# Float32 products for the first two chunks, unsplit until later, and weights first in the queue: attention and rational feed-forward on one core

## The chip, the core and the metric

The kernel runs on one core of a Trainium2 chip. Its engines are TensorE (PE in the profile, its weight loads PEld), VectorE (DVE), ScalarE (ACT), GpSimd (POOL) and SyncE (SP, which issues all transfers). Each runs its own list of instructions in order. The metric is device time in microseconds: the median of three runs before the change is 1022.39 us (1021.11 to 1024.19).

## The reference

```python
# q, k, v: 8 batches x 8 heads x 576 positions x 64;  w_in 512 x 2048;  w_out 2048 x 512
scores = q @ k.T / sqrt(64);  only positions rel in [0, 64) back count (window 64)
x = softmax(scores) @ v                     # heads side by side: 4608 tokens x 512
h = x @ w_in                                # 4608 x 2048
P = a[0] + a[1]*h + a[2]*h**2 + a[3]*h**3
Q = 1 + abs(b[0])*abs(h) + abs(b[1])*h**2
out = (P / (Q + 1e-6)) @ w_out              # 4608 x 512
```

The weights arrive as 64-bit floats, seen by the kernel as pairs of 32-bit words.

## The kernel before, in words

**Tiling.** The 4608 tokens are cut into 12 chunks of 384 (`CH`). A chunk's attention is done in four units, one for each pair of heads: `unit_load` (transfers of q, k, v), `unit_scores` (scores in PSUM, mask and scale on VectorE, exponentials on ScalarE, one scaling by the reciprocal sums: `sm`), `unit_transpose` (`pT`), `unit_av` (the product with v in PSUM `ps_x`, copied to `x`). The 2048 hidden columns are cut into 16 blocks. One block of one chunk is a step: `ffn1` multiplies the chunk's `x` (four tiles of 128 x 384) with a block of `w_in` into `h`, then works out the gate P/Q on ScalarE, VectorE and, from the 29th gate on (`DEC`), one operation on GpSimd; `ffn2` multiplies the gate with a block of `w_out` and adds it up in three PSUM tiles `o` of 128 x 512 over all steps of a chunk. `ffn2` runs three steps behind `ffn1` (`LAG`).

**Order of steps.** Steps 0 to 7 are the first 8 blocks of chunk 0, steps 8 to 15 the same of chunk 1, 16 to 23 the second half of chunk 1, 24 to 31 the second half of chunk 0. The half sum of chunk 0 is therefore set aside after step 7 (three copies to `part`, line 287, on ScalarE) and added at the end of step 31. From step 32 on each chunk takes 16 steps, to step 191.

**Products in parts.** Every operand is split into a high part rounded to `float32r` and a low part, the rest. A product is made of three `float32r` matmuls: high by low, high by high, low by high. So a step has 12 first products (128 x 384) and 9 second ones (128 x 512). `x` is split in `unit_av` (a cast on ScalarE, a subtraction on VectorE, `xl`), the gate by three more operations on VectorE, the weights by `decode`.

**Decoding weights.** `decode` loads a tile of 512 KB into a staging buffer `w_st` (two of them) and turns 64-bit floats into 32-bit ones: an absolute value on ScalarE (line 113), a maximum, a shift, two merges on VectorE (lines 114 to 118), then the split: a cast on ScalarE (line 121) and a subtraction on VectorE (line 122). There are 16 tiles of `w_in` and 16 of `w_out`. Four `w_in` tiles are loaded while the first chunk's units are done; the others are called step by step from a table, `todo`, which is filled by `at(step, function, ...)`.

**What sets the order.** The program is written step by step, but a scheduler of the framework then sets the order of each engine's instructions by its own estimate of times. Since each engine works in order, an instruction that waits holds all behind it on its engine.

Of the kernel before, what the change touches and what calls it, by code (L numbers as in the profile page):

```python
# [20 lines left out]
DEC = 28  # L21
AHEAD = 3
LAG = 3
W_AT = 0, 1, 2, 3
WLEAD = len(W_AT)
# [6 lines left out]
def swa_rational_ffn(ctx: ExitStack, tc: tile.TileContext, qT, kT, v, w_in, w_out, a, b, out):  # L32
# [17 lines left out]
    xp = ctx.enter_context(tc.tile_pool(name="xp", bufs=2))  # L50
    tmp = ctx.enter_context(tc.tile_pool(name="tmp", bufs=2))
    gp = ctx.enter_context(tc.tile_pool(name="gp", bufs=LAG + 1))
    op = ctx.enter_context(tc.tile_pool(name="op", bufs=2))
# [13 lines left out]
    def make_mask():  # L67
        nc.gpsimd.memset(mask, BIG)
        for j in range(NM):
            for half in range(2):  # L70
# [23 lines left out]
    wi_h = const.tile([P, NCC, DFF], F32R, name="wi_h")  # L94
    wi_l = const.tile([P, NCC, DFF], F32R, name="wi_l")
    wo_h = const.tile([P, NF, DO], F32R, name="wo_h")
    wo_l = const.tile([P, NF, DO], F32R, name="wo_l")
# [3 lines left out]
    def decode(src, hi, lo):  # L101

        w = stage.tile([P, 512, 2], U32, name="w_st", bufs=2)
        if len(src.shape) == 3:
            nc.sync.dma_start(out=w.rearrange("p (c n) two -> p c (n two)", c=src.shape[1]), in_=src)
        else:
            nc.sync.dma_start(out=w.rearrange("p n two -> p (n two)"), in_=src)
        low, high = w[:, :, 0], w[:, :, 1]
        c = stage.tile([P, 512], U32, name="w_c")
        cf = c.bitcast(F32)  # L110


        nc.scalar.activation(cf, w.bitcast(F32)[:, :, 1], AF.Abs)
        nc.vector.tensor_scalar(out=cf, in0=cf, scalar1=2.0 ** -15, scalar2=None, op0=ALU.max)

        nc.vector.tensor_scalar(out=c, in0=c, scalar1=3, scalar2=0x3FFFFFF8, op0=ALU.logical_shift_left, op1=ALU.bitwise_and)
        nc.vector.scalar_tensor_tensor(out=c, in0=low, scalar=29, in1=c, op0=ALU.logical_shift_right, op1=ALU.bitwise_or)  # L117
        nc.vector.scalar_tensor_tensor(out=c, in0=high, scalar=0xC0000000, in1=c, op0=ALU.bitwise_and, op1=ALU.bitwise_or)  # L118
        if len(hi.shape) == 3:
            cf = cf.rearrange("p (c n) -> p c n", c=hi.shape[1])  # L120
        nc.scalar.copy(out=hi, in_=cf)
        nc.vector.tensor_tensor(out=lo, in0=cf, in1=hi.bitcast(F32), op=ALU.subtract)

    def load_w_in(i):
        sl = slice(i * P, (i + 1) * P)
        decode(w_in_v[:, :, 2 * i * P:2 * (i + 1) * P], wi_h[:, :, sl], wi_l[:, :, sl])

    def load_w_out(i):
        decode(w_out_v[:, i, :], wo_h[:, i, :], wo_l[:, i, :])
# [87 lines left out]
    def unit_av(c, hp):  # L217
# [7 lines left out]
        xh[c, hp] = xp.tile([P, CH], F32R, name=f"xh{hp}")  # L225
        xl[c, hp] = xp.tile([P, CH], F32R, name=f"xl{hp}")
        x = ps.rearrange("p t s -> p (t s)")
        nc.scalar.copy(out=xh[c, hp], in_=x)
# [5 lines left out]
    def ffn1(c, i):  # L234
        h = ps_h.tile([P, CH], F32, name="h")
        n = 0
        for cc in range(NCC):
            for w, x in ((wi_h, xl), (wi_h, xh), (wi_l, xh)):
                nc.tensor.matmul(h, w[:, cc, i * P:(i + 1) * P], x[c, cc], start=n == 0, stop=n == 3 * NCC - 1)  # L239
                n += 1  # L240
# [3 lines left out]
        gh = gp.tile([P, CH], F32R, name="gh")  # L244
        gl = gp.tile([P, CH], F32R, name="gl")
# [8 lines left out]

        nc.scalar.activation(ah, u, AF.Ln, bias=QADD)
        nc.scalar.activation(ah, ah, AF.Exp, scale=-1.0)  # L256
        nc.vector.scalar_tensor_tensor(out=gh, in0=num, scalar=a_sb[:, 0:1], in1=ah, op0=ALU.add, op1=ALU.mult)  # L257
# [12 lines left out]
    def ffn2(s):  # L270
# [6 lines left out]
        for t in range(NTS):  # L277
            ts = slice(t * P, (t + 1) * P)
            for n, (g, w) in enumerate(((gl, wo_h), (gh, wo_l), (gh, wo_h))):
                nc.tensor.matmul(acc[c][t], g[:, ts], w[:, i, :], start=first and n == 0, stop=last and n == 2)  # L280
# [3 lines left out]
        if c == 0 and c not in part:  # L284
            part[c] = const.tile([P, NTS, DO], F32, name="part")
            for t in range(NTS):
                nc.scalar.copy(out=part[c][:, t, :], in_=o[t])
            return
        for t in range(NTS):
            ob = part[0][:, t, :] if s == total - 1 else op.tile([P, DO], F32, name="ob")  # L290
            if c in part:
                nc.vector.tensor_tensor(out=ob, in0=o[t], in1=part[c][:, t, :], op=ALU.add)
# [15 lines left out]
    wi, wo = list(range(H, NF)), list(range(H, NF))  # L308
    queue = [(load_w_in, wi.pop(0)) for _ in range(WLEAD)]
    while wi or wo:  # L310
        if wi:
            queue.append((load_w_in, wi.pop(0)))
        queue.append((load_w_out, wo.pop(0)))
    for n, call in enumerate(queue):
        at(H + n - 1, *call)

# [16 lines left out]

    for k in range(NU + 2):
# [7 lines left out]
        if k in W_AT:  # L342
            load_w_in(W_AT.index(k))
# [45 lines left out]
```

## Time and profile before

| | |
|---|---|
| median of three runs | 1022.39 us |
| profiled execution, its own time | 1025.14 us |
| its span | 1023.3 us |
| TensorE busy | 953.1 us (93%) |
| VectorE busy | 850.3 us (83%) |
| ScalarE busy | 725.8 us (71%) |
| GpSimd busy | 233.7 us (23%) |
| transfers | 64.09 MB, mean 63 GB/s |
| mean granted TensorE clock | 0.978 |

Busy shares are means over stages with different limits, so they are read by stretches of time. In rows of single instructions the columns are the start and the length in us, then engine, line, operation, output and inputs with their shapes, and how many such instructions follow each other (x24). An instruction's length overlaps the next one's; the cost of one in a full queue is the distance from its start to the next start. In the rows of groups the numbers behind the bar are the sum of busy time and the mean length in ns.

### The profile page before, as it was taken

How to read it: one execution, taken by the hardware profiler on the slowest of the kernel's cores; microseconds unless marked ns; L12 is line 12 of the kernel's file. 1: busy time of each engine (PE TensorE's matmuls, PEld its weight loads, DVE VectorE, ACT ScalarE, POOL GpSimd, SP SyncE). 2: the span in 40 equal slices, each digit the busy share in tenths (PEclk: the TensorE clock that was granted, in tenths of full speed). 3: DMA queues.
4: the chain of work that ended last, by engine and by line, in shares of the span. 5: the costliest groups of instructions: out<-in, count | busy, mean ns of one | idle time of the engine just before them, and what ended most of it. 6: DMA issues, size and time to landing. Idle time of an engine off the chain costs nothing.

```text
span 1023.3 us, 18244 instructions
## 1 busy us (share of the span) xinstructions
PE 953.1 (93%) x6624; PEld 840.4 (82%) x6624; DVE 850.3 (83%) x1639; ACT 725.8 (71%) x1734; POOL 233.7 (23%) x231
## 2 busy tenths in 40 slices
PE   2677876899999999999999999999999999999997
PEld 2565755788898898898898898898898898888996
DVE  5999999998878878878878878878888888888785
ACT  4675765577767867867867867867867867866664
POOL 2000010002322322322322322322322322322221
PEclk9878989899999999999999999999999999999999
DMA  6634433111112112111112112111112112100000
GB/s 197 205 99 133 133 94 111 50 50 55 60 30 60 61 31 65 64 31 58 60 30 61 61 31 65 64 32 58 60 31 60 62 31 65 65 16 2 31 1 31
DMA packets 68537, 64.09 MB, mean 63 GB/s; under 512 B 4448, under 2 KB 61792, under 8 KB 68448
## 3 DMA queue, kind: packets, MB, share of 16 engines
q1 hardware_dynamic: 68448, 62.93, 19.8%
q8 instruction: 52, 0.85, 0.4%
q14 instruction: 37, 0.30, 0.1%
HBM read 53.48 MB, written 9.44 MB: 61 GB/s over the span
## 4 chain that ended last, share of the span: by engine, by line
PE 81%; DVE 11%; ACT 3%; DMA 3%; issue 1%; POOL 0%; SPq 0%; POOLq 0%; ACTq 0%; DVEq 0%
PE o L280 37%; PE h L239 35%; PE ps_x L223 3%; PE ps_s L182 3%; PE ps_s L212 3%; DMA w_st<-w_in 1%; DVE w_c L117 1%; DMA w_st<-w_out 1%; ACT sm L201 1%; DVE w_c L118 1%; DVE num L259 1%; DVE gh L257 1%; DVE u L258 1%; DVE num L249 1%; DVE num L250 1%
## 5 line engine op out<-in xcount | busy, mean ns | idle before, releaser
L239 PE MATMUL h<-xl,wi_h 128*128 128x384 f32 x768 | 264.9, 345 | 14.8 <-DVE num L250 8.6
L239 PE MATMUL h<-xh,wi_h 128*128 128x384 f32 x768 | 260.6, 339 | 0.0
L239 PE MATMUL h<-xh,wi_l 128*128 128x384 f32 x768 | 259.7, 338 | 0.0
L280 PE MATMUL o<-wo_h,gl 128*128 128x512 f32 x576 | 238.1, 413 | 22.3 <-DVE gl L260 22.3
L252 POOL TENSOR_TENSOR u<-u,ah 128x384 f32<-128x384 f32 x164 | 166.7, 1017 | 317.3 <-ACT u L248 278.7
L280 PE MATMUL o<-wo_h,gh 128*128 128x512 f32 x576 | 231.7, 402 | 0.0
L280 PE MATMUL o<-wo_l,gh 128*128 128x512 f32 x576 | 230.2, 400 | 0.0
L249 DVE TENSOR_TENSOR num<-num,h 128x384 f32<-128x384 f32 x192 | 106.1, 553 | 108.9 <-ACT num L247 108.7
L246 ACT ACTIVATE ah<-h 128x384 f32<-128x384 f32 x192 | 94.3, 491 | 108.1 <-PE h L239 83.3
L205 POOL TENSOR_TENSOR sm<-sm,rs 128x768 f32<-128x768 f32 x40 | 61.7, 1541 | 457.9 <-DVE rs L204 352.3
L201 ACT ACTIVATE sm<-sm,nmx 128x128 f32<-128x128 f32 x288 | 111.9, 390 | 76.4 <-DVE nmx L198 76.4
L239 PEld LDWEIGHTS h<-xl,wi_h 128*128 128x128 f32 x768 | 145.4, 189 | 23.3 <-DVE num L250 11.3
L280 PEld LDWEIGHTS o<-wo_h,gl 128*128 128x128 f32 x576 | 111.3, 193 | 51.3 <-DVE gl L260 24.6
L239 PEld LDWEIGHTS h<-xh,wi_h 128*128 128x128 f32 x768 | 145.5, 189 | 4.6
L239 PEld LDWEIGHTS h<-xh,wi_l 128*128 128x128 f32 x768 | 145.4, 189 | 0.0
L248 ACT ACTIVATE u<-ah,b_sb 128x384 f32<-128x384 f32 x192 | 135.4, 706 | 0.0
L280 PEld LDWEIGHTS o<-wo_h,gh 128*128 128x128 f32 x576 | 111.2, 193 | 26.1
L257 DVE SCALAR_TENSOR_TENSOR gh<-num,a_sb,ah 128x384 fp32r<-128x384 f32 x192 | 114.8, 615 | 17.6 <-ACT ah L256 16.9
L247 ACT ACTIVATE num<-h,a_sb 128x384 f32<-128x384 f32 x192 | 128.2, 668 | 0.0
L280 PEld LDWEIGHTS o<-wo_l,gh 128*128 128x128 f32 x576 | 111.8, 194 | 19.4
L250 DVE SCALAR_TENSOR_TENSOR num<-num,a_sb,h 128x384 f32<-128x384 f32 x192 | 117.9, 614 | 5.9
L259 DVE SCALAR_TENSOR_TENSOR num<-num,a_sb,u 128x384 f32<-128x384 f32 x192 | 115.8, 620 | 0.8
(45 smaller groups left out, 1090.3 us busy)
## 6 DMA issues: line engine op xcount, KB each, us to landing
out<-ob SPq DMA_DIRECT2D x33, 256.0 KB, 2.0
w_st<-w_in SPq DMA_DIRECT2D x16, 512.0 KB, 4.4
w_st<-w_out SPq DMA_DIRECT2D x16, 512.0 KB, 3.6
q<-qT SPq DMA_DIRECT2D x32, 192.0 KB, 3.3
vt<-v SPq DMA_DIRECT2D x16, 384.0 KB, 3.4
vt<-v SPq DMA_DIRECT2D x16, 320.0 KB, 3.9
kt<-kT SPq DMA_DIRECT2D x16, 224.0 KB, 3.6
kt<-kT SPq DMA_DIRECT2D x16, 192.0 KB, 3.6
```

Of the source, the lines that this page charges most:

```text
L201: nc.scalar.activation(sm[:, j, :], sm[:, j, :], AF.Exp, bias=nmx[:, j:j + 1], accum_out=sums[:, j:j + 1])
L205: (nc.vector if c < 2 else nc.gpsimd).tensor_tensor(out=sm, in0=sm, in1=rs.unsqueeze(2).broadcast_to([P, NR, P]), op=ALU.mult)
L239: nc.tensor.matmul(h, w[:, cc, i * P:(i + 1) * P], x[c, cc], start=n == 0, stop=n == 3 * NCC - 1)
L246: nc.scalar.activation(ah, h, AF.Abs)
L247: nc.scalar.activation(num, h, AF.Identity, scale=a_sb[:, 3:4], bias=a_sb[:, 2:3])
L248: nc.scalar.activation(u, ah, AF.Identity, scale=b_sb[:, 1:2], bias=b_sb[:, 0:1])
L249: nc.vector.tensor_tensor(out=num, in0=num, in1=h, op=ALU.mult)
L250: nc.vector.scalar_tensor_tensor(out=num, in0=num, scalar=a_sb[:, 1:2], in1=h, op0=ALU.add, op1=ALU.mult)
L252: (nc.vector if n_gates[0] <= DEC else nc.gpsimd).tensor_tensor(out=u, in0=u, in1=ah, op=ALU.mult)
L257: nc.vector.scalar_tensor_tensor(out=gh, in0=num, scalar=a_sb[:, 0:1], in1=ah, op0=ALU.add, op1=ALU.mult)
L259: nc.vector.scalar_tensor_tensor(out=num, in0=num, scalar=a_sb[:, 0:1], in1=u, op0=ALU.add, op1=ALU.subtract)
L280: nc.tensor.matmul(acc[c][t], g[:, ts], w[:, i, :], start=first and n == 0, stop=last and n == 2)
```

## The change

For the chunks 0 and 1 (`c < NX`, steps 0 to 31) each product is one matmul of float32 operands, 4 first and 3 second products to a step, with `x`, gate and weights unsplit. The gate, which before formed its low part with the reciprocal's error, now refines the reciprocal by two operations (`u` twice) and is one float32 tile. Weights are decoded into float32 tiles. They are split later by `split`, called one tile a step from step 14 to step 45 (`SPLIT`), for the chunks from 2 on. Staging has three buffers. The first `w_in` tile is loaded ahead of the first unit. The mask is filled block by block. Tiles come from shared pools, and the last output uses the pool `op`.

```diff
+NX = 2
+SPLIT = 14
-W_AT = 0, 1, 2, 3
-WLEAD = len(W_AT)
+W_AT = 0, 1, 2
+WLEAD = 1 + len(W_AT)
...
-    def decode(src, hi, lo):
+    def decode(src, dst):
-        w = stage.tile([P, 512, 2], U32, name="w_st", bufs=2)
+        w = stage.tile([P, 512, 2], U32, name="w_st", bufs=3)
...
-        nc.scalar.copy(out=hi, in_=cf)
-        nc.vector.tensor_tensor(out=lo, in0=cf, in1=hi.bitcast(F32), op=ALU.subtract)
...
+    def split(w, name):
+        hi = wp.tile(list(w.shape), F32R, name=name + "_h", tag="w")
+        lo = wp.tile(list(w.shape), F32R, name=name + "_l", tag="w")
+        nc.scalar.copy(out=hi, in_=w)
+        nc.vector.tensor_tensor(out=lo, in0=w, in1=hi.bitcast(F32), op=ALU.subtract)
+        return hi, lo
...
+        if c < NX:
+            xh[c, hp] = xp.tile([P, CH], F32, name="x", tag="x")
+            nc.scalar.copy(out=xh[c, hp], in_=x)
+            return
...
+            if c < NX:
+                nc.tensor.matmul(h, wi[i][:, cc, :], xh[c, cc], start=cc == 0, stop=cc == NCC - 1)
+                continue
...
+        if c < NX:
+            nc.vector.scalar_tensor_tensor(out=u, in0=u, scalar=QADD, in1=ah, op0=ALU.add, op1=ALU.mult)
+            nc.vector.scalar_tensor_tensor(out=u, in0=u, scalar=2.0, in1=ah, op0=ALU.subtract, op1=ALU.mult, reverse0=True)
+            g = gp.tile([P, CH], F32, name="g", tag="g")
+            nc.vector.scalar_tensor_tensor(out=g, in0=num, scalar=a_sb[:, 0:1], in1=u, op0=ALU.add, op1=ALU.mult)
+            gs[c, i] = g, None
+            return
...
+            if c < NX:
+                nc.tensor.matmul(acc[c][t], gh[:, ts], wo[i], start=first, stop=last)
+                continue
...
-            part[c] = const.tile([P, NTS, DO], F32, name="part")
+            part[c] = [wp.tile([P, DO], F32, name="part", tag="w") for _ in range(NTS)]
...
+    for i in range(NF):
+        at(SPLIT + 2 * i, split_w_in, i)
+        at(SPLIT + 2 * i + 1, split_w_out, i)
...
+    load_w_in(0)
     for k in range(NU + 2):
...
-            load_w_in(W_AT.index(k))
+            load_w_in(1 + W_AT.index(k))
```

The scheduler orders the changed program anew on every engine. Three places matter below. In the rows a tile's name stands without its number; lines are those of each kernel's own file: in the changed one 115 is the decode's absolute value, 116 to 120 its four operations on VectorE, 134 and 135 the split, 214 the exponentials, 268 to 280 the gate, 320 the copies of the half sum.

ScalarE at the half sum of chunk 0. Before (line 287 is the copy, 113 the absolute value of a weight tile, 255 a logarithm of a gate):

```order
L248 ACTIVATE u<-ah,b_sb 128x384
L201 ACTIVATE sm,sums<-sm,nmx 128x128
L287 COPY part<-o_880 128x512
L201 ACTIVATE sm,sums<-sm,nmx 128x128 x5
L255 ACTIVATE ah<-u 128x384
L287 COPY part<-o_881 128x512
L287 COPY part<-o_882 128x512
L113 ACTIVATE w_c<-w_st 128x512
L255 ACTIVATE ah<-u 128x384
```

Now:

```order
L274 ACTIVATE ah<-ah 128x384
L227 COPY pT<-ps_s 128x768
L320 COPY part<-o_805 128x512
L320 COPY part<-o_806 128x512
L320 COPY part<-o_807 128x512
L115 ACTIVATE wi<-w_st 128x512
L115 ACTIVATE wo<-w_st 128x512
L115 ACTIVATE wi<-w_st 128x512
```

The three copies now stand together, ahead of the absolute values of three weight tiles, with no gate's work in between.

VectorE at the same place, behind the gate of step 7. Before, around the first decode operation behind the copies (line 114, the second row here, takes the absolute value that follows the copies):

```order
L118 SCALAR_TENSOR_TENSOR w_c<-w_st,w_c 128x512
L114 TENSOR_SCALAR w_c<-w_c 128x512
L116 TENSOR_SCALAR w_c<-w_c 128x512
L257 SCALAR_TENSOR_TENSOR gh<-num,a_sb,ah 128x384
L117 SCALAR_TENSOR_TENSOR w_c<-w_st,w_c 128x512
L122 TENSOR_TENSOR wi_l<-w_c,wi_h 128x4x128
```

Now:

```order
L278 SCALAR_TENSOR_TENSOR u<-u,ah 128x384
L280 SCALAR_TENSOR_TENSOR g<-num,a_sb,u 128x384
L116 TENSOR_SCALAR wi<-wi 128x512
L118 TENSOR_SCALAR wi<-wi 128x512
L116 TENSOR_SCALAR wo<-wo 128x512
L119 SCALAR_TENSOR_TENSOR wi<-w_st,wi 128x512
L116 TENSOR_SCALAR wi<-wi 128x512
L118 TENSOR_SCALAR wo<-wo 128x512
L205 SCALAR_TENSOR_TENSOR sm<-ps_s,mask 128x384 x2
```

VectorE's next work behind step 7's gate is the decode of those three tiles, and the mask of chunk 1's last unit stands behind their first operations.

VectorE at the gate of step 10. Before (its last operation, line 260, is the seventh row):

```order
L118 SCALAR_TENSOR_TENSOR w_c<-w_st,w_c 128x512
L122 TENSOR_TENSOR wo_l<-w_c,wo_h 128x512
L259 SCALAR_TENSOR_TENSOR num<-num,a_sb,u 128x384
L204 RECIPROCAL rs<-sums 128x6
L257 SCALAR_TENSOR_TENSOR gh<-num,a_sb,ah 128x384
L122 TENSOR_TENSOR wi_l<-w_c,wi_h 128x4x128
L260 TENSOR_TENSOR gl<-num,ah 128x384
```

Now (its last operation, line 280, is the last row):

```order
L135 TENSOR_TENSOR wi_l<-wi,wi_h 128x512
L277 SCALAR_TENSOR_TENSOR u<-u,ah 128x384
L135 TENSOR_TENSOR wo_l<-wo,wo_h 128x512
L269 SCALAR_TENSOR_TENSOR num<-num,a_sb,h 128x384
L135 TENSOR_TENSOR wi_l<-wi,wi_h 128x512
L120 SCALAR_TENSOR_TENSOR wo<-w_st,wo 128x512
L135 TENSOR_TENSOR wo_l<-wo,wo_h 128x512
L277 SCALAR_TENSOR_TENSOR u<-u,ah 128x384
L278 SCALAR_TENSOR_TENSOR u<-u,ah 128x384
L216 TENSOR_SCALAR sums<-sums 128x6
L278 SCALAR_TENSOR_TENSOR u<-u,ah 128x384
L280 SCALAR_TENSOR_TENSOR g<-num,a_sb,u 128x384
```

Splits that the code calls at steps 14 and later stand among the operations of step 10's gate. In all, between step 7's gate and this row VectorE now has 12 decodes, 18 splits, the rest of one attention unit and two more masks with their maxima, and the gates of steps 8 to 11 but for one operation.

At the head of the program, SyncE's first transfers were q, k, v of the first unit and then `w_st`; now `w_st` comes first and q, k, v of the first unit next, then the second `w_st`. VectorE's first rows were one decode operation and the first unit's masks; now they are the four decode operations of the first tile, one of the second tile, and then those masks.

More of the change, by code (lines that the diff above doesn't have):

```diff
@@ L278, in ffn2 @@
             ts = slice(t * P, (t + 1) * P)
-            for n, (g, w) in enumerate(((gl, wo_h), (gh, wo_l), (gh, wo_h))):
-                nc.tensor.matmul(acc[c][t], g[:, ts], w[:, i, :], start=first and n == 0, stop=last and n == 2)
+            if c < NX:
+                nc.tensor.matmul(acc[c][t], gh[:, ts], wo[i], start=first, stop=last)
+                continue
+            hi, lo = wo[i]
+            for n, (g, w) in enumerate(((gl, hi), (gh, lo), (gh, hi))):
+                nc.tensor.matmul(acc[c][t], g[:, ts], w, start=first and n == 0, stop=last and n == 2)
         if not last:
@@ L307, in swa_rational_ffn @@
         at(i, load_w_out, i)
[L308 to L313, printed above, removed]
+    left_in, left_out = list(range(H, NF)), list(range(H, NF))
+    queue = [(load_w_in, left_in.pop(0)) for _ in range(WLEAD)]
+    while left_in or left_out:
+        if left_in:
+            queue.append((load_w_in, left_in.pop(0)))
+        queue.append((load_w_out, left_out.pop(0)))
     for n, call in enumerate(queue):
         at(H + n - 1, *call)
+    for i in range(NF):
+        at(SPLIT + 2 * i, split_w_in, i)
+        at(SPLIT + 2 * i + 1, split_w_out, i)
     start = {}
```

55 lines of the change are left out of this document (29 added, 26 removed).

## The prediction

> **What bounds the kernel now.** I read the stretches of time first, then the chain that ended last, then single instructions where the chain changes engine. The stretches (columns: us, then busy us and instructions of PE, PEld, DVE, ACT and POOL, then the granted clock, DMA share, GB/s):
>
> ```profile
> 0.00:30.00 30.00, 10.57 (x112) 8.56 (x113) 19.63 (x39) 14.85 (x48) 6.88 (x27) 1.00 0.67 202
> 90.00:120.00 30.00, 24.21 (x185) 20.66 (x185) 29.97 (x62) 19.29 (x46) 0.00 (x0) 0.89 0.48 146
> 120.00:150.00 30.00, 21.41 (x136) 17.43 (x135) 29.03 (x60) 21.05 (x54) 5.63 (x2) 0.91 0.31 98
> 150.00:180.00 30.00, 21.74 (x118) 17.25 (x117) 28.60 (x56) 17.78 (x41) 1.59 (x1) 0.96 0.33 102
> 180.00:210.00 30.00, 25.68 (x116) 22.40 (x115) 29.25 (x58) 18.47 (x36) 0.00 (x0) 0.91 0.12 36
> 210.00:240.00 30.00, 30.00 (x207) 26.13 (x206) 26.61 (x54) 22.29 (x52) 1.12 (x1) 1.00 0.20 64
> ```
>
> Up to 210 us VectorE is the full engine (in the 120 us from 90 on it idles 3.2 us) while TensorE waits at a reduced clock; from 210 us TensorE is full. The chain of waits shows the place where the bound changes hands:
>
> ```profile
> 2.11 5.60 DMA w_st<-w_in
> ...
> 65.68 5.99 PE o L280 x18
> ...
> 201.64 0.48 DVE gl L260
> 202.25 4.38 PE o L280 x18
> 206.63 4.19 PE h L239 x24
> ...
> 239.41 4.12 PE o L280 x18
> ```
>
> At 202.25 us, with the second products of step 18, the chain leaves VectorE and stays on TensorE until the end: 1023.3 - 202.25 = 821.0 us of TensorE's queue. So the new time is: when TensorE can start its last unbroken run in the changed kernel, plus what it then still has to do. I work out both against this one execution.
>
> **The price of a float32 product.** No float32 product of 384 or 512 columns was profiled. Float32 products of attention were:
>
> ```profile
> L223 PE MATMUL ps_x<-pT,vt 128*64 128x64 f32 x1152 | 45.7, 230 | 3.8 <-ACT pT L214 3.8
> ```
>
> ```profile
> 21.44 1.55 PE L223 MATMUL ps_x<-pT,vt 128*64 128x64 f32 x24
> ...
> 44.87 0.92 PE L223 MATMUL ps_x<-pT,vt 128*64 128x64 f32 x24
> ...
> 57.25 0.52 PE L239 MATMUL h<-xh,wi_l 128*128 128x384 f32 x1
> 57.57 0.52 PE L239 MATMUL h<-xl,wi_h 128*128 128x384 f32 x1
> ...
> 193.94 0.63 PE L280 MATMUL o<-wo_h,gh 128*128 128x512 f32 x1
> 194.36 0.63 PE L280 MATMUL o<-wo_h,gl 128*128 128x512 f32 x1
> ```
>
> The code issues 12 such products per unit and 48 units, 576; the trace has 1152 records, so two for each. The last four rows are float32r products while the clock was halved: 0.32 us apart at 384 columns, 0.42 to 0.43 at 512; at the full clock the chain has 24 in 4.19 us (0.174 each) and 18 in 4.12 us (0.229). Is a float32 record one such pass or two? The 24 records of a unit run in two halves of the array, 12 in a row, of 64 columns. They took 1.55 us at the halved clock and 0.92 at the full one, so 0.63 us scale with the clock. One pass of 64 columns saves 64/384 x 0.16 = 0.027 us when the clock doubles, 12 of them 0.32; two passes save 0.64. It is two. A float32 product is therefore four passes. Ends: 4 x 0.16 (half the cold spacing) = 0.64 us and 4 x 0.174 = 0.70 us at 384 columns; 0.853 and 0.92 at 512. I take the middle, 0.668 and 0.886, since two passes share a weight load. Against three float32r products (0.522 and 0.69) a step's 4 first products rise from 2.09 to 2.67 us and its 3 second ones from 2.07 to 2.66: 1.17 us of TensorE more per step, in 32 steps.
>
> The Trainium skill ("FP8 and Floating Point Precision", TensorE Precision Notes) also counts four passes for true float32, and its page "TensorE: Matmul & The Clock Gate" (the section on the 56 ns gap) gives a warm pass N / 2.4 GHz + 2.5 ns. By these pages the estimate is 0.65 and 0.863 us, and the sum below would end near 1037 us; the trace's own spacing of 0.174 is 7% above the page's, and I stay with it.
>
> **What VectorE saves, and where it puts the time.** Its prices are read from one start to the next:
>
> ```profile
> 94.86 0.42 DVE L116 TENSOR_SCALAR w_c<-w_c 128x512 uint32<-128x512 uint32 x1
> 95.19 0.61 DVE L259 SCALAR_TENSOR_TENSOR num<-num,a_sb,u 128x384 f32<-128x384 f32 x1
> 95.73 0.55 DVE L229 TENSOR_TENSOR xl<-ps_x,xh 128x384 fp32r<-128x384 f32 x1
> 96.19 0.42 DVE L116 TENSOR_SCALAR w_c<-w_c 128x512 uint32<-128x512 uint32 x1
> 96.53 0.62 DVE L259 SCALAR_TENSOR_TENSOR num<-num,a_sb,u 128x384 f32<-128x384 f32 x1
> 97.05 0.69 DVE L117 SCALAR_TENSOR_TENSOR w_c<-w_st,w_c 128x512 uint32<-128x512 uint32 x1
> 97.66 1.02 DVE L192 SCALAR_TENSOR_TENSOR sm<-ps_s,mask 128x384 f32<-128x384 f32 x2
> 98.59 0.55 DVE L260 TENSOR_TENSOR gl<-num,ah 128x384 fp32r<-128x384 f32 x1
> ```
>
> So 0.46 to 0.47 for a 384-column operation, 0.53 with a coefficient tile, 0.33 for a TENSOR_SCALAR of 512, 0.60 for the other 512-column ones, 0.47 per half mask. A gate loses one operation net (0.53 x 32 = 17 us), eight units lose `xl` (8 x 0.47 = 3.8 us). A tile's decode costs 2 x 0.33 + 2 x 0.60 = 1.87 us instead of 2.48; but its split (0.60) is only moved. The moved splits decide: the order puts 18 of the 32 ahead of step 10's gate, and decodes of tiles for steps 16 and later with them.
>
> I follow the new order.
> (1) The first second-product starts at 65.68 us now. Ahead of it VectorE drops 11 splits (6.6 us) and 4 `xl` (1.9), does five more decodes (less a piece, 8.2) and a gate shorter by 1.5: -1.8 us. The first weight transfer is 1.4 us earlier (0.74 for 2.11), but the second tile's first operation now stands ahead of the first masks, and three buffers let bursts of loads wait on each other: +0.8. Start: 64.7 us (bounds 62 and 68; the 10.4 us that VectorE idles in the first 30 us are mostly transfers, which stay). The masks' five memsets are on POOL, idle after its 6.88 us; no one waits for the last block before 8 us: nothing either way, 0.4 us at most.
> (2) From there TensorE has, until the last second product of step 7: 24 second products x 0.886, 20 first products x 0.668, and five attention pieces of 0.7 to 0.85: 21.3 + 13.4 + 3.8 = 38.5 us, so 103.2. VectorE has only 30.6 us up to step 7's gate (95.3) and then stands at a decode whose absolute value ScalarE takes after the three copies of the half sum.
>
> ```profile
> 122.64 1.06 ACT L287 COPY part<-o 128x512 f32<-128x512 f32 x2
> 123.59 0.68 ACT L113 ACTIVATE w_c<-w_st 128x512 f32<-128x512 f32 x1
> 124.16 0.52 ACT L255 ACTIVATE ah<-u 128x384 f32<-128x384 f32 x1
> ...
> w_st<-w_in SPq DMA_DIRECT2D x16, 512.0 KB, 4.4
> ```
>
> (3) Three copies at 0.475 and one absolute value at 0.57 make 2.0: VectorE resumes at 105.2, having lost 10 us. This wait is new: in the kernel before, softmax and gate work stood between and the copies delayed it by half a microsecond.
> (4) From there to step 10's gate VectorE's queue holds 12 decodes (22.5), 18 splits (10.8), the rest of chunk 1's last unit and two units of chunk 2 (7.2) and four gates less one operation (11.2): 51.7 us, so 156.9.
> (5) Waits within: a staging buffer is refilled 4.4 us after its release, then 0.57 of ScalarE; with 12 decodes nearly in a row on three buffers some show. Bounds: 0, and 8 us (two refills). I take 3.6, a little over the 3.2 us that VectorE idled in the 120 us above. Step 10's gate is ready at 160.5, and TensorE, which has emptied its queue by then, starts the run: 41.75 us earlier than 202.25.
> (6) What is left on TensorE then. Before, from step 18's second products: 170 steps' first products, 174 steps' second. Now from step 10's: 18 float32 steps of first products and 160 split, 22 and 160 of second. The difference is 18 x 2.67 - 10 x 2.09 = 27.2, 22 x 2.66 - 14 x 2.07 = 29.5, and one score and two transpose groups, 2.4: +59.1 us. The 14 splits left fall under that run: VectorE's gate is ready well ahead of TensorE at each later step (its queue from step 10 to 31 holds 71 us, TensorE's 115).
>
> Sum: 1023.3 + 59.1 - 41.75 = 1040.7 us of span. The profiled execution took 1025.14, 1.84 over its span and 2.75 over the median of 1022.39; against that median I forecast 1040.
>
> **Rivals.**
> A (ends faster): a float32 product costs no more than the three it replaces, 0.522 and 0.69. Then the 34.7 us of float32 in (2) and the 106.6 us in (6) shrink by 22%, 31 us: 1009. It decides from 12% below my price on (0.59 and 0.78), where 17.4 us are gone; that is under four passes of 0.16. Against it stand the two clocks above. One page speaks for it: the Trainium skill ("TensorE: Matmul & The Clock Gate", Part 3) says that a weight load overlaps running products only where row groups differ; with its 107 ns load in the open, an estimate from the page makes 2 x (0.32 + 0.107) against 3 x (0.16 + 0.107), 7% dearer only, and the time near 1017. The trace is against it:
>
> ```profile
> L239 PEld LDWEIGHTS h<-xh,wi_h 128*128 128x128 f32 x768 | 145.5, 189 | 4.6
> ```
>
> A load of 189 ns lies in a spacing of 174, so loads are hidden.
> B: VectorE comes to the decode of (3) late (a transfer of 4.4 us not covered in (1) or (2), twice), so it loses no 10 us there beyond what it lost before; step 10's gate comes at 151: 1031.
> C: the pauses of TensorE between 105 and 160 let its clock fall, as in the rows at 193.94, and VectorE or ScalarE must wait for first products at half speed: three pairs at 5.3 us, half of each lost: +8, 1048.
> D: nothing to see: price at its low end (-5.9 us), no waits in (5) (-3.6), and B's 9 us together: 1022.
>
> **How the numbers follow.** The sum itself 0.60, with its own range 1033 to 1047 (price +-5.9, (1) +-3, (5) -3.6 and +4.4); B 0.18; C 0.11; D 0.05; A 0.06. What a measurement of this kernel can tell from no change is about 0.3%, 3 us. Faster 0.06 (A), same 0.05 (D), slower 0.89. Leaving A, D and the outer half of C out, the range is 1026 to 1050.
>
> **What would show it.** Right: float32 first products with two records each about 0.33 us apart; VectorE idle for about 10 us near 95 to 105 us, released by ScalarE's absolute value of a tile; TensorE full from about 160 us, but steps up to 31 about 5.3 us long. Wrong: 0.26 us between records or less (A); the idle time at the half-sum copies gone (B); or a chain that leaves VectorE well before 145 us or after 170.

## The result, and the profile after

The changed kernel takes 1051.76 us (median; 1051.66 to 1052.59), the kernel before 1022.13 us in the same comparison: a ratio of 1.0278, 95% interval 1.0259 to 1.0297. It is slower, as forecast, but by 29.6 us where the forecast had 17.6, and the time lies 1.8 us above the range. The profiled execution took 1051.66 us with a span of 1049.9. It lies at its median, while the profiled execution of before took 1025.14, 3.0 us above the 1022.13 of this comparison: so 26.6 us of the 29.6 show in the two spans, and the rest is that difference.

The stretches of time after the change, at the places shown before (columns as there: us, then busy us and instructions of PE, PEld, DVE, ACT, POOL, then granted clock, DMA share, GB/s):

```profile
90.00:120.00 30.00, 22.15 (x109) 11.90 (x107) 20.76 (x43) 16.10 (x45) 0.00 (x0) 0.93 0.31 98
120.00:150.00 30.00, 16.62 (x125) 10.80 (x125) 28.04 (x55) 20.94 (x49) 1.72 (x1) 0.67 0.47 146
150.00:180.00 30.00, 24.84 (x73) 12.11 (x72) 28.84 (x54) 21.54 (x50) 1.73 (x1) 1.00 0.05 16
180.00:210.00 30.00, 30.00 (x102) 15.05 (x101) 17.98 (x34) 13.86 (x28) 0.00 (x0) 1.00 0.05 14
```

VectorE, full between 90 and 120 us before, now idles 9 us there; TensorE has only 16.6 of 30 us to do in the next stretch, at a clock of 0.67; and from 180 us TensorE is full, 30 us earlier than before, but on float32 products. The chain of waits (the work that ended last, each piece with its start and length in us) shows the points on which the forecast was built:

```profile
44.44 4.82 DMA w_st<-w_in
...
51.07 4.08 DMA w_st<-w_out
...
69.50 5.42 PE o L309 x12
...
76.58 5.16 PE h L256 x16
...
93.91 5.15 PE o L309 x12
...
102.30 5.16 PE o L309 x12
...
107.48 0.59 ACT part L320
108.07 0.58 ACT wi L115
...
108.67 0.44 DVE wi L116
...
164.94 0.62 DVE g L280
165.60 5.42 PE o L309 x12
171.01 0.66 PE ps_s L225 x6
171.67 5.16 PE h L256 x16
176.83 2.58 PE o L309 x6
179.67 2.77 PE o L309 x6
```

Second products start at 69.50 us. TensorE works through the first eight steps until 107.48. Then the half sum is copied, ScalarE takes the absolute value of a tile, and only then VectorE goes on, at 108.67. For the next 57 us, to step 10's gate, the chain is mostly VectorE's, with two staging transfers of 3.7 us and a softmax on ScalarE among it, and at 165.60 TensorE begins its run. The waits of VectorE for decoded tiles up to 250 us (engine, line, what it waited for: us in all, times, longest) hold the hole of 8.0 us:

```profile
DVE wi L116 <- ACT wi L115: 25.5, 9, 8.0
```

The larger part of this sum comes earlier. Up to the first second product (65.7 us before, 69.5 after) the same wait was and is:

```profile
DVE w_c L114 <- ACT w_c L113: 10.8, 4, 8.4
DVE wi L116 <- ACT wi L115: 15.4, 6, 5.1
```

What the forecast did not look at is the stage whose code did not change. Chunks 4 to 9 take 77.30 us each where they took 76.85 (from the start of ScalarE's first absolute value of `h` of a chunk to that of the next). The chain in a steady chunk, before:

```profile
604.22 4.13 PE o L280 x18
608.36 0.66 PE ps_s L212 x6
609.01 4.24 PE h L239 x24
613.25 0.85 PE ps_x L223 x24
614.10 0.82 PE ps_s L182 x24
```

and after:

```profile
605.73 1.64 DVE gl L289
607.41 2.35 PE o L313 x9
...
624.85 4.12 PE o L313 x18
628.97 1.93 PE h L260 x11
630.90 0.66 PE ps_s L225 x6
631.56 2.28 PE h L260 x13
633.83 2.09 PE o L313 x9
635.92 0.85 PE ps_x L236 x24
```

Before, the transposes (`ps_s` x6) come right behind 18 second products and 24 first products follow in one piece. After, they stand inside the first products, between 11 and 13, and the attention product `ps_x` behind second ones. Once in a chunk the chain then runs over VectorE, which it did in no steady chunk before. What TensorE waits for there, from 432 to 985 us:

```profile
PE o L313 <- DVE gl L289: 1.2, 7, 0.2
```

At that place two products start 0.56 us apart (606.85 and 607.41) where the ones around them follow at 0.23: 0.33 of the 0.45 us by which a chunk is longer. VectorE is late there because this `gl` takes 1.71 us, beside an operation of GpSimd; in chunks 4 to 9 of the kernel before no `gl` takes more than 0.56 (the rows are in the last section).

### The profile page after: what moved, and what is told of

Its sections match the earlier page's. It is cut to its first block, busy times and chain, and to the rows that moved or that the text cites. A ratio compares the mean times of both kernels' runs of the same rounds, so it can differ in the third digit from the quotient of the medians.

```text
span 1049.9 us, 17764 instructions
## 1 busy us (share of the span) xinstructions
PE 981.6 (93%) x6400; PEld 796.5 (76%) x6400; DVE 871.3 (83%) x1599; ACT 715.9 (68%) x1734; POOL 250.1 (24%) x235
## 4 chain that ended last, share of the span: by engine, by line
PE 70%; DVE 17%; ACT 5%; DMA 4%; issue 3%; POOL 1%; SPq 0%; POOLq 0%; DVEq 0%; ACTq 0%
PE h L260 25%; PE o L313 24%; PE o L309 7%; PE h L256 6%; PE ps_x L236 3%; PE ps_s L195 3%; DVE gl L289 2%; DMA w_st<-w_in 2%; PE ps_s L225 2%; DVE num L288 2%; DVE gh L286 2%; DVE u L287 2%; ACT sm L214 1%; DVE sm L205 1%; DMA w_st<-w_out 1%
## 5 line engine op out<-in xcount | busy, mean ns | idle before, releaser
L271 POOL TENSOR_TENSOR u<-u,ah 128x384 f32<-128x384 f32 x164 | 183.3, 1124 | 326.1 <-ACT u L267 241.0
L260 PE MATMUL h<-xl,wi_h 128*128 128x384 f32 x640 | 219.8, 343 | 0.4 <-DVE num L269 0.4
L260 PE MATMUL h<-xh,wi_l 128*128 128x384 f32 x640 | 217.7, 340 | 0.0
L260 PE MATMUL h<-xh,wi_h 128*128 128x384 f32 x640 | 214.9, 336 | 0.0
L313 PE MATMUL o<-wo_h,gl 128*128 128x512 f32 x480 | 188.3, 392 | 4.9 <-DVE gl L289 4.8
L313 PE MATMUL o<-wo_h,gh 128*128 128x512 f32 x480 | 189.6, 395 | 0.0
L313 PE MATMUL o<-wo_l,gh 128*128 128x512 f32 x480 | 189.0, 394 | 0.0
L273 ACT ACTIVATE ah<-u 128x384 f32<-128x384 f32 x192 | 100.5, 524 | 54.8 <-POOL u L271 47.1
L260 PEld LDWEIGHTS h<-xh,wi_h 128*128 128x128 f32 x640 | 120.2, 188 | 3.6
L260 PEld LDWEIGHTS h<-xh,wi_l 128*128 128x128 f32 x640 | 120.1, 188 | 0.0
L256 PE MATMUL h<-x,wi 128*128 128x384 f32 x256 | 94.9, 521 | 21.6 <-DVE num L269 17.0
## 6 DMA issues: line engine op xcount, KB each, us to landing
out<-ob SPq DMA_DIRECT2D x36, 256.0 KB, 2.1
```

Of the source, the lines that this page charges most:

```text
L256: nc.tensor.matmul(h, wi[i][:, cc, :], xh[c, cc], start=cc == 0, stop=cc == NCC - 1)
L260: nc.tensor.matmul(h, w[:, cc, :], x[c, cc], start=n == 0, stop=n == 3 * NCC - 1)
L271: (nc.vector if n_gates[0] <= DEC else nc.gpsimd).tensor_tensor(out=u, in0=u, in1=ah, op=ALU.mult)
L313: nc.tensor.matmul(acc[c][t], g[:, ts], w, start=first and n == 0, stop=last and n == 2)
```

## The experiments

Each run was timed beside the kernel before. The table reads the traces: when ScalarE takes the first absolute value of step 32 (the first step of chunk 2, up to which all float32 first products and nearly all second ones are done), the length of a steady chunk, and what follows from the start of the last chunk to the end. These three come from one execution each; that of the kernel before took 2 to 3 us more than its medians, so differences to it of that size are not read.

| run | median us | ratio, 95% interval | step 32 | chunk | last chunk, end |
|---|---|---|---|---|---|
| before | 1022.4 | | 256.8 | 76.85 | 75.7 |
| the change | 1051.8 | 1.0278 (1.0259 to 1.0297) | 278.6 | 77.30 | 77.4 |
| split_at_load | 1034.65 | 1.0108 (1.0093 to 1.0123) | 254.6 | 78.00 | 80.4 |
| split_kept | 1047.72 | 1.0230 (1.0210 to 1.0251) | 265.6 | 78.01 | 77.9 |
| both_kept | 1038.91 | 1.0148 (1.0131 to 1.0165) | 258.5 | 78.01 | 79.1 |
| shared_pools | 1032.49 | 1.0095 (1.0077 to 1.0113) | 256.9 | 77.83 | 79.5 |
| change_own_pools | 1046.32 | 1.0234 (1.0211 to 1.0256) | 276.4 | 77.02 | 74.3 |
| load_own_pools | 1028.51 | 1.0048 (1.0033 to 1.0064) | 256.7 | 77.03 | 77.2 |
| kept_own_pools | 1023.06 | 0.9999 (0.9990 to 1.0008) | 254.2 | 76.79 | 77.6 |
| kept_from_13th | 1025.09 | 1.0016 (1.0004 to 1.0027) | 256.0 | 76.79 | 78.5 |
| kept_from_21st | 1031.79 | 1.0079 (1.0062 to 1.0096) | 263.3 | 76.79 | 77.7 |
| loads_3_earlier | 1053.56 | 1.0290 (1.0274 to 1.0306) | 271.2 | 78.01 | 79.1 |
| kept_loads_3_earlier | 1028.63 | 1.0049 (1.0035 to 1.0063) | 260.6 | 76.79 | 76.9 |
| load_kept_own_pools | 1039.23 | 1.0146 (1.0128 to 1.0164) | 270.2 | 77.03 | 77.2 |

**split_at_load: the float32 products undone, the rest kept.** Each tile is split right behind its decode (the output pool has two buffers again, and the weight pool three more).

```diff
-NX = 2
+NX = 0
@@ load_w_in, load_w_out
+        split_w_in(i)
...
+        split_w_out(i)
@@
-    for i in range(NF):
-        at(SPLIT + 2 * i, split_w_in, i)
-        at(SPLIT + 2 * i + 1, split_w_out, i)
```

> Float32 products undone for chunks 0 and 1 (split operands everywhere, each tile split right after its decode); the first weight tile at the queue's head, three staging buffers, masks block by block and the pools stay. Theory (the loss is the float32 products together with the work that the new order moves ahead of the gates of steps 8 to 11): back to the time before, 1016 to 1028 us, TensorE's last run starting near 200 us. Rival (the weights ahead of q, k and v and bursts of three loads delay the start): 4 to 6 us slower than before, 1026 to 1030, with the first second product at 69 us or later instead of 65.7.

The time misses the theory and the rival: step 32 begins 2.2 us earlier than before and the first second product comes at 61.8 us, so nothing is lost at the start; yet the run is 1.1% slower. In the spans, chunks 2 to 10 take 6.9 us more together (chunks 4 to 9 78.0 each), and the last chunk with the end 4.7. A loss remains when no float32 product is left, and it sits in unchanged code.

**split_kept and both_kept: the order put back.** In the first the split's cast and subtraction are kept at the place in the program where they are written, in the second the decodes from the ninth tile on as well, by a call that takes an instruction out of the scheduler's hands.

```diff
 def split(w, name):
-        nc.scalar.copy(out=hi, in_=w)
-        nc.vector.tensor_tensor(out=lo, in0=w, in1=hi.bitcast(F32), op=ALU.subtract)
+        tc.keep_in_program_order(nc.scalar.copy(out=hi, in_=w))
+        tc.keep_in_program_order(nc.vector.tensor_tensor(out=lo, in0=w, in1=hi.bitcast(F32), op=ALU.subtract))
```

> As changed, float32 products kept, but each split is held behind the work written ahead of it on its engine, so that it is issued at its step (14 to 45) and not earlier. Theory: the gates of steps 8 to 11 lose the 18 splits and, since the order is made anew, 8 decodes ahead of them: step 8's gate at about 128 us instead of 149, TensorE's last run from there with 868 + 28 us: span near 1025, time 1020 to 1033. Rival (the float32 price alone, about 1.0 us of TensorE in each of 32 steps, makes the slowdown): unchanged within 3 us, 1049 to 1055.

> As the kernel with the splits held, and every decode from the ninth tile on is held at its place in the code too (its absolute value on ScalarE and its first operation on VectorE). Theory: the first gate has 35 us of VectorE work ahead of it instead of 50, step 9's gate 90 instead of 116; TensorE's last run starts at 110 to 118 us with 866 + 28 us left: 1004 to 1020 us, faster than before the change. Rival (float32 price alone): 1049 to 1055. Second rival (held decodes wait for their transfers one by one, which the pulled-forward order hid): 1025 to 1040.

With the splits in their places step 32 begins 13.0 us earlier than in the change, with the decodes too 20.1 us earlier: of the 22 us by which the change begins it late, 20 are the order and not the products. Both times miss the theory's ranges, by 15 and 19 us, since much of it is given back later, with chunks of 78.0 us and a chunk 2 of 80.6 us. (1038.9 lies in the second rival's range, but step 32 begins 7.1 us earlier than with the decodes free, so held decodes are not what costs.)

**shared_pools: one part of the change alone, on the kernel before.** The pools of `x` and of the gate are shared instead of one for each name.

```diff
-    xp = ctx.enter_context(tc.tile_pool(name="xp", bufs=2))
+    xp = ctx.enter_context(tc.tile_pool(name="xp", bufs=16))
...
-        xh[c, hp] = xp.tile([P, CH], F32R, name=f"xh{hp}")
+        xh[c, hp] = xp.tile([P, CH], F32R, name="xh", tag="x")
...
-        gh = gp.tile([P, CH], F32R, name="gh")
+        gh = gp.tile([P, CH], F32R, name="gh", tag="g")
```

> The kernel before with one thing of the change: xh and xl of all head pairs share one pool of 16 buffers, gh and gl one pool of 8, where they had pools by name. Theory: these pools alone make the scheduler cut the first and second products of the steady chunks around the transposes in another way, and a chunk takes about 78.0 us where it took 76.85, as in the run that split each tile at its load: 10 chunks by 0.9 to 1.2, so 1031 to 1035 us, with step 32 begun within 2 us of before's 256.8. Rival: the longer chunks there come from the third staging buffer, the half sums or the weight tiles, and this run stays at 1021 to 1024 us with chunks of 76.8.

0.95% slower, with the start unmoved: the theory holds. No instruction is added, none is longer in the code, the buffers are as many as before; but any buffer may now serve any tile, and the scheduler's order for TensorE is another one (that it reckons with the buffers is my reading; the runs show only that the order changes). Its chain in a steady chunk:

```profile
642.58 1.04 PE h L239 x6
643.63 0.66 PE ps_s L212 x6
644.28 1.06 PE h L239 x6
645.37 0.49 ACT ah L246
...
657.68 0.58 ACT ob L294
658.30 3.03 PE o L280 x12
```

For 13 us of each chunk the chain leaves TensorE for ScalarE and VectorE, to the copies of the finished sums (`ob`), which come behind the gates. TensorE then stands still for 0.74 us, of the 0.98 by which a chunk is longer.

**change_own_pools: the change with pools by name.**

```diff
-        xh[c, hp] = xp.tile([P, CH], F32R, name="xh", tag="x")
+        xh[c, hp] = xp.tile([P, CH], F32R, name="xh", tag=f"xh{hp}")
...
-        gl = gp.tile([P, CH], F32R, name="gl", tag="g")
+        gl = gp.tile([P, CH], F32R, name="gl", tag="gl")
```

> The changed kernel whole, except that x and g get pools by name again (the float32 x shares the two buffers of xh of its head pair, the float32 g the four of gh). Theory: the chunks come back from 77.3 to 76.85 us and the last one from 64.6 to 60.0 up to its last gate, while step 32 begins at 276 to 281 us as before: 1051.8 less 3 to 6, 1045 to 1049 us. Rival: the longer chunks come from VectorE and GpSimd lying beside each other (gh 695 ns against 615, u 1147 against 1016), whatever the pools: 1050 to 1053 us.

5.4 us less than the change, as the theory's sum had it, but not where it put them. Of the 6.3 us between the two spans 2.2 come before step 32 (276.4), only 1.0 in chunks 2 to 10 together, and 3.1 in the last chunk and the end. Chunks 4 to 9 come to 77.02 us, and TensorE no longer waits in them; chunk 2 takes 78.4 instead of 76.8 and gives most of that back.

**load_own_pools: no float32 and pools by name.** The kernel of split_at_load with the same edit.

> The run that split each tile at its load (no float32 products; the head's order, the block-wise masks, three staging buffers and the in-place decode kept) with pools by name. Theory: its start stays 2 us ahead of before and its chunks come to 76.85 us: 1018 to 1022 us, faster than before by 0 to 0.4%. Rival: the pools are not what made its chunks 78.0 us: 1031 to 1036 us.

6.1 us less than split_at_load, but 5.4 us more than before, where I expected it a little faster. Both sayings miss by half: pools are a part. What the rest is was not settled. Chunks 2 to 10 take 0.8 us more together than before and the end 1.5; so the profiled spans, 1025.5 and 1023.3, differ by 2.2, less than the medians do, since the profiled execution of before is a late one.

**kept_own_pools: float32 with both cures.** The decodes from the ninth tile on and all splits at their places, pools by name, and the splits of the first eight tiles begun at step 14, one tile of each matrix a step, the others' from step 28.

```diff
+        keep = tc.keep_in_program_order if loaded[0] >= 8 else (lambda x: x)
...
+        keep(nc.scalar.activation(cf, high.bitcast(F32), AF.Abs))
+        keep(nc.vector.tensor_scalar(out=cf, in0=cf, scalar1=2.0 ** -15, scalar2=None, op0=ALU.max))
...
-        at(SPLIT + 2 * i, split_w_in, i)
-        at(SPLIT + 2 * i + 1, split_w_out, i)
+        at(14 + i if i < 8 else 20 + i, split_w_in, i)
+        at(16 + i if i < 8 else 20 + i, split_w_out, i)
```

> The changed kernel with float32 products, but the decodes from the ninth tile on and all splits kept at the place in the program where they are written, pools by name, and the splits of the first eight tiles at steps 14 to 23 and of the others at steps 28 to 35 two or three per step. Theory: what float32 itself costs when nothing is put ahead of the gates is 1 to 4 us at step 32 (256.8 before), and with chunks of 76.85 us the time is 1022 to 1029 us. Rival: the price of the float32 products (about 0.12 and 0.17 us on each of the 192 and 96 pieces) cannot be hidden whatever the order, and it ends at 1035 to 1042 us.

1023.06 us, the kernel before to within a tenth of a per cent. All 128 first and 96 second float32 products (not 192 and 96, as the expectation has it) are in it at their full price, and no net loss is left in the time. Its stretches:

```profile
90.00:120.00 30.00, 28.69 (x121) 14.64 (x122) 28.29 (x61) 21.29 (x55) 0.00 (x0) 1.00 0.45 142
120.00:150.00 30.00, 28.39 (x105) 14.20 (x104) 28.38 (x57) 18.51 (x36) 1.92 (x1) 1.00 0.49 153
150.00:180.00 30.00, 30.00 (x95) 15.16 (x94) 28.93 (x57) 21.10 (x49) 1.47 (x1) 1.00 0.23 72
180.00:210.00 30.00, 28.09 (x124) 14.28 (x123) 30.00 (x61) 22.45 (x51) 3.33 (x1) 1.00 0.18 57
```

From 90 to 210 us the change's TensorE has 93.6 us of work and its VectorE 95.6; here both are busy, 115.2 and 115.6. The dearer products run while VectorE is nearly full anyway.

**load_kept_own_pools: the same pins without float32.** The kernel of load_own_pools with decodes and splits from the ninth tile on kept in program order.

> The run with no float32 products at all, each tile split at its load, pools by name (1028.5 us), with its decodes and splits from the ninth tile on kept in program order. It tells what float32 by itself does once the order is the same as in the kept run with float32 (1023.1 us). If keeping the order is worth the whole gain and the float32 products only cost their price, this run is faster than that: 1012 to 1019 us. If float32 with late splits is what frees VectorE in the first 250 us (32 splits of about 1.2 us there, taken off it until step 14), this run stays behind it: 1024 to 1031 us.

1039.2 us: 16 us slower than the run with float32 in the same manner of order, and 11 us slower than where the scheduler was free. So the second case has the right direction, and the time lies 8 us beyond its range: with every split done at its load, TensorE has 21.7 us of work between 210 and 240 us while VectorE is full:

```profile
210.00:240.00 30.00, 21.71 (x153) 17.66 (x151) 29.97 (x59) 21.26 (x49) 2.85 (x1) 0.89 0.22 67
```

Float32 products are what allows splits to wait until TensorE is the bound; pins with every split at its load only hurt. The two runs differ in the products and in the splits' place at once, and no run parts the two: split products need the split tiles.

**kept_from_21st and kept_from_13th: where in the start the order costs.** As kept_own_pools, with the first twenty or the first twelve decodes left to the scheduler.

```diff
-        keep = tc.keep_in_program_order if loaded[0] >= 8 else (lambda x: x)
+        keep = tc.keep_in_program_order if loaded[0] >= 20 else (lambda x: x)
```

> The same with the first twenty decodes left free, so that VectorE's order up to step 7 is the changed kernel's (16 decodes ahead of the first second product, 20 ahead of step 7), and only the eleven decodes and eighteen splits that stood ahead of gates 8 to 11 there are back in their places. It prices that block alone. Theory (the block is most of the loss at the start, 20 us of the 22 that step 32 came late): step 32 at 256 to 266 us, 1023 to 1033 us in all. Rival (the 16 decodes ahead of the first gate are what cost): step 32 at 270 to 278 us, 1037 to 1046 us.

> The run with float32 products, pools by name and everything from the ninth tile on kept in program order (1023.1 us, as before), with the ninth to twelfth decode left free. There TensorE stood still for 8.9 us at 69 to 78 us and VectorE for 4.4 and 1.4 us, behind a decode at its pinned place. Theory: four more decodes are done in VectorE's early gaps, the run of TensorE from 90 us on starts sooner, 1016 to 1021 us. Rival: the nine microseconds are chunk 1's softmax, which comes when it comes, and the four decodes only delay the first gates by 7.5 us of VectorE's work: 1022 to 1030 us.

With the first twenty free, VectorE's order up to step 7 is that of the change, and only the block of 12 decodes (the expectation says eleven) and 18 splits ahead of the gates 8 to 11 is back in its places: 1031.8 us, 14.5 less than change_own_pools (the splits' later schedule is in this difference), as the theory had it. Step 12's absolute value comes at 141.7 us; in the change it was 164.5. The remaining 8.7 us to kept_own_pools are the decodes ahead of the first gates: the first second product comes at 70.8 us here, at 63.6 with twelve free and at 55.4 with eight. kept_from_13th came out on the rival's side: four more free decodes fill no gap (VectorE idles 18.1 us ahead of the first second product where it idled 18.3), they delay the first gates by 8.2 us, and cost about 2 us in all. In kept_own_pools the gap itself stands in TensorE's waits up to 300 us as transposes that wait for the softmax:

```profile
PE ps_s L229 <- DVE sm L222: 14.5, 2, 8.9
```

**loads_3_earlier and kept_loads_3_earlier: the hole at the half sum.** The later tiles' loads are called earlier, by two steps in the first (the words "three steps" in its expectation are a slip; the index given there is what ran) and by three in the second.

```diff
-        at(H + n - 1, *call)
+        at(H + n - 3, *call)
```

> The changed kernel with one line moved: the later tiles' loads (those of the second half of DFF) stand three steps ahead of their old place plus nothing else (step H + n - 3 instead of H + n - 1). Two more tiles are then decoded ahead of the copies of the half sums, into the 8.1 us in which VectorE waits for them, and the run of 10 decodes with 18 splits that stood ahead of gate 10 is spread to gate 12. Theory (the wait for the half sums lies on the path that ends in the late start of step 10): VectorE resumes at the same 108.7, has 58 us of work up to gate 12 where it had 52 up to gate 10, and TensorE has 12.6 us less left there: 5 to 8 us less, 1043.5 to 1047 us. Rival (TensorE's float32 products from step 8 on set the time, the wait hides beside them): 1050 to 1053 us.

> The run with float32 products, decodes and splits kept in program order and pools by name (1023.1 us, as before), with the later tiles' loads moved ahead by three steps. It stands at TensorE 19.9 of 30 us busy between 60 and 90 us and VectorE 20.8, and waits there for staging transfers and Abs of later tiles (16 us in all); with decodes standing ready, theory: up to a third of that comes back, 1016 to 1021 us. Rival: those gaps are attention's (the transposes wait 14.5 us for the softmax on VectorE), more decodes there only delay it: 1022 to 1027 us.

The first does at the start what the theory said: step 32 begins 7.4 us earlier, VectorE's waits for decoded tiles (up to 280 us, as they stand in the row below) fall by a third, and TensorE's run starts at step 12 instead of 10:

```profile
DVE wi L116 <- ACT wi L115: 16.9, 7, 5.4
```

```profile
111.85 0.58 ACT part L320
112.44 0.56 ACT wi L115
...
170.86 0.54 DVE g L280
171.44 8.03 PE o L309 x12
```

Yet the time is not less: 1.8 us more, with intervals that overlap. The order of the steady chunks is another one too: chunk 2 takes 80.4 us, the others 78.0, some 10 us given back. The wait lies on the chain in the change's own trace, and the earlier step 32 agrees with that; it does not prove it, since the copies come 4.4 us later here and other work has moved as well. The time alone would have hidden the gain. Under the pins the same edit, by three steps, costs 5.6 us, past the rival's range too, all of it before step 32: there the copies of the half sum come at 138.7 us instead of 123.0, behind the decodes moved ahead of them.

## Why the prediction was wrong, point by point

The forecast of the span was 1040.7, the measured one 1049.9, 9.2 more. (The median is 11.8 above the forecast, since the change's profiled execution does not lie above its median as that of before did.)

- **(1) Start of the second products**: 64.7 forecast, 69.50 measured, 4.8 of the miss and out of its bounds. I allowed 0.8 us for loads that wait on each other; this allowance is the step that failed. VectorE's work there is as forecast, 1.8 us less than before (51.98 us against 53.74), but it idles 17.5 us where it idled 11.9. Those 5.6 us are the 0.8 and the whole miss. The rise is in the waits for decoded tiles, and the chain has two staging transfers close behind each other there, 4.82 and 4.08 us. kept_own_pools, with eight decodes there, starts at 55.4, but idles 18.3: it is earlier by less work, not by less waiting.
- **(2) TensorE to the end of step 7**: 38.5 forecast, 107.48 - 69.50 = 38.0 measured. The price in it was 3.5% too high: 5.16 us for 16 records (eight products) is 0.645 a first product, 5.15 for six second products 0.858, against 0.668 and 0.886. Both lie at the low ends I had named. This saves 1.1 us; about 0.6 of it is taken back, mostly by pieces of 12 that take longer than 5.15 (the one at 69.50 takes 5.42) and by attention. The Trainium skill ("TensorE: Matmul & The Clock Gate", "Wait — 56ns, not 53.3ns?") gives a warm pass from which the prediction had an estimate of 0.65 and 0.863; the trace agrees with it within 1%, and the row of float32r products that I preferred did not carry over.
- **(3) The hole at the half sum**: 2.0 us until VectorE goes on, 1.2 measured; 10 us lost, 8.0 measured. Right in kind: the chain runs through it. Only the last of the three copies counts, since the other two start at 105.77 and 106.63, while TensorE still works.
- **(4) and (5) VectorE from there to step 10's gate**: 55.3 forecast, 165.60 - 108.67 = 56.9 measured, 53.9 of it work (51.7 forecast) and 3.0 idle (3.6). Right, with the 12 decodes and 18 splits in front of it; putting these back in their places, together with the splits' later schedule, is worth 14.5 us in kept_from_21st.
- **(6) What is then left on TensorE**: 59.1 us more than before forecast, 63.2 measured (1049.9 - 165.60 against 821.05). This is the step that failed in its reasoning. The lower price took off 18 x 4 x 0.023 + 22 x 3 x 0.028 = 3.5. Against it the steady chunks cost 3.1 us more, the last one and the end 1.7, and the rest, 2.8, lies in the float32 stretch. There 12 second products in two pieces of 6 take 5.6 us (176.83 to 182.44) where one piece of 12 takes 5.15, three times over; that is half of it, and the other half stays open. I counted the products of chunks 2 to 11 and let them keep their pace, since their code is the same. That is the term I put at nothing. What the runs show in its place is a new order of the steady chunks, in which TensorE waits once a chunk for a `gl` that takes three times as long with GpSimd's operation beside it: 0.33 us in each of seven chunks, 2.3 of the 3.1. The shared pools in the diff change that order: they cost 9.4 us on the kernel before (shared_pools) and 5.4 us in the change (change_own_pools), where by name this wait is gone. But the chunks 2 to 10 lose only 1.0 us by it in all, so the pools are not the whole reason for the 3.1. My sentence that VectorE's gates stand ready well ahead of TensorE at each later step failed as well, behind step 31: between 283 and 375 us the chain is off TensorE, and at 375.50 TensorE waits 1.5 us for a `gl`.

The rivals: A's price fell with the records. B and D needed a VectorE that does not wait at the half sum, and it waited 8.0 us there. C came in part: in the stretch from 120 us the clock is 0.67, but no product of TensorE is on the chain between 107.48 and 165.60.

Beyond the sum, the runs change what the loss is put down to. The forecast booked float32 as 59.1 us of more TensorE work against an earlier start; so it reads as a price. Taken one after the other from the change, the medians go from 1051.8 to 1046.3 (pools), 1031.8 (the block ahead of gates 8 to 11), 1025.1 and 1023.1 (decodes ahead of the first gates), with every float32 product still there: the loss is order, the deferred splits' steps included, and not the price of the products. In the other direction float32 with the late splits that it allows, in a kept order, is worth 16 us against splitting at load. What stays open: why load_own_pools keeps 5.4 us, the part of the steady chunks that pools by name do not give back, and how much of (1) would go with transfers in another order, which was not tried.

## What to carry to other kernels

Where a scheduler sets the order, a change of pools or of a load's step can change every later stage: compare the order of the steady stage, not only of the place that was edited, and give it a term of its own. Deferred work (here splits) must be held at its place, or the scheduler may put much of it in front of the next gate, as it did here with 18 of 32. But holding alone can also hurt, as load_kept_own_pools shows. And a dearer operation on an engine that waits can be free as long as what it replaces leaves the engine that is full; read which engine is full in that stretch before pricing it.

## What the hardware showed that was not expected

A float32 record of 384 columns takes 5.16 / 16 = 0.322 us, two passes of 0.161, while float32r products of the same columns follow each other at 0.174 at the full clock (the prediction's row of 24). 0.161 is half of the 0.32 that they take at the halved clock, so the 0.013 us that a float32r product has on top at the full clock is not there in a float32 pass.

VectorE's and GpSimd's operations lengthen where a new order lays them over each other in some ways. The groups `gh` on VectorE and `u` on GpSimd (behind the bar: busy us, mean ns), before, and after:

```profile
L252 POOL TENSOR_TENSOR u<-u,ah 128x384 f32<-128x384 f32 x164 | 166.7, 1017 | 317.3 <-ACT u L248 278.7
...
L257 DVE SCALAR_TENSOR_TENSOR gh<-num,a_sb,ah 128x384 fp32r<-128x384 f32 x192 | 114.8, 615 | 17.6 <-ACT ah L256 16.9
```

```profile
L271 POOL TENSOR_TENSOR u<-u,ah 128x384 f32<-128x384 f32 x164 | 183.3, 1124 | 326.1 <-ACT u L267 241.0
...
L286 DVE SCALAR_TENSOR_TENSOR gh<-num,a_sb,ah 128x384 fp32r<-128x384 f32 x160 | 110.0, 687 | 38.9 <-ACT ah L274 38.1
```

The means grow by about a tenth, 615 to 687 and 1017 to 1124 ns; in kept_own_pools, whose chunks take 76.79 us, they are 619 and 1022. The mean hides two kinds. In chunks 4 to 9 after the change the 72 `gh` with no operation of GpSimd beside them take 612 ns, and the 24 with `u` beside them 943. The longest is the `gl` on which TensorE waits:

```profile
605.47 1.47 POOL L218 TENSOR_TENSOR sm<-sm,rs 128x768 f32<-128x768 f32 x1 [5.67 <-DVE rs L217]
605.64 1.71 DVE L289 TENSOR_TENSOR gl<-num,ah 128x384 fp32r<-128x384 f32 x1
```

It begins 0.17 us into GpSimd's scaling of the softmax and ends 0.41 us behind that operation's end; elsewhere a `gl` takes 0.55. Lying beside each other is not enough: before, 23 `gh` begin in the last 0.1 us of a `u` and take 619 ns. The Trainium skill ("SBUF — State Buffer", "Who interferes with whom") says that a VectorE operation with two inputs in SBUF contends with a GpSimd operation that reads SBUF, since its second input comes through the read interface that the two share. The trace agrees for these rows, though other pairs of such operations lie over each other here without a loss.
